# Channel attention and a squared-ReLU network on one core: the squares of batches 2 to 4 are summed by accumulating transfers instead of VectorE additions

## The chip, the cores and the metric

The kernel runs on one core of a Trainium2 chip. TensorE (PE) multiplies matrices, VectorE (DVE) and ScalarE (ACT) work elementwise, GpSimd (POOL) and SyncE (SP) here do little but issue transfers, which 16 DMA engines carry out. The metric is the device time of one execution in microseconds; three executions of the kernel before took 2157.32 to 2159.95 us, median 2158.8.

## What is computed

For each of four batches q, k and v are 6080 x 256. The columns of q and k are normalised over the 6080 rows, a 256 x 256 matrix of scores is made and put through a softmax, v is multiplied with it, and the result goes through two layers of 256 x 2048 and 2048 x 256 with a squared ReLU between them:

```python
qn = q / (np.linalg.norm(q, axis=1, keepdims=True) + 1e-06)
kn = k / (np.linalg.norm(k, axis=1, keepdims=True) + 1e-06)
s = kn.transpose(0, 2, 1) @ qn / tau
s = s - s.max(-1, keepdims=True)
a = np.exp(s)
a /= a.sum(-1, keepdims=True) + 1e-09
x = (v @ a).reshape(B * S, D)
r = np.maximum(x @ w_in, 0.0)
out = (r * r) @ w_out
```

The part that the change touches is the sum of squares inside the two norms: for each batch, 512 columns (256 of k, 256 of q), each summed over 6080 rows, which the host pads to 6144 = 128 x 48.

## The kernel before

**Tiles.** Batch b's q and k stand in one array of 128 partitions by 48 row blocks by 512 columns. `score_load` (L137) brings two row blocks at a time, a tile of 128 x 1024 values and 512 KB, on SyncE's queue; so a batch has 24 such tiles. `score_norm` (L144) squares a tile on ScalarE (L152) into a tile `sq` and VectorE adds it to the batch's running sum `acc` of 128 x 1024 (L153); the first tile of a batch is squared straight into `acc` (L149). That makes 23 squares and 23 additions in each batch. `score_split` (L155) splits the same tile for the score matmuls. `norms` (L197) adds the two halves of `acc` on VectorE (L199) and sums over the partitions on TensorE (L202); everything of the batch's attention follows from it.

**Buffers.** `sq` has the pool `work` with two buffers, and these two serve other steps under the same tag: the sums of weights in `weight_sums` (L508, its tile `f`), the combined tiles of `combine_sums` (L298), and the decoded weights at the start. A tile gets its buffer when all that read the buffer's last tile are done.

**Stages.** Batch 1's squares stand at the very start, before anything else can run. From then on the main loop goes through 192 quads (24 chunks of v by 8 pairs of hidden blocks); each quad is 7 products (m1 to m7, L440 to L498, matmuls at L384 of three passes each) and up to 8 products of the second layer (L550). m1 writes a bank that ScalarE copies (L447); m6 then adds to that same bank (L449), so it must follow the copy. m3's bank is evacuated by ScalarE (L394). ScalarE squares and casts (L395, L396, L418), VectorE subtracts the rounded part (L397, L419) and adds m7 (L472).

**Side work.** The attention of batches 2 to 4 is laid between the quads of the batch before, by a table of due times in quads (L705 to L733): `score_norm` of tile i is due 0.8 of a quad ahead of its matmuls; batch 2's first twelve are spread over quads 9 to 17 and the rest over quads 17 to 28, those of batches 3 and 4 over some 27 quads each, and `norms` 2 to 3 quads behind the last. `tie` (L769) keeps a side instruction from moving more than one quad ahead on TensorE, ScalarE and VectorE; within that, a scheduler sets the order on each engine, and every engine works its own list in order.

**GpSimd's queue.** Before the change it carries weights only: `wsc` (the folded weights, L318), `wins` and `wop` at the start, and in quads 9 to 13 the stores of `weight_sums` (L529), six for each of three weight blocks: `wodM` and `wos`, partly read from a tile `wo`, partly from a tile `hl` that VectorE has just made (L526).

Of the kernel before, what the change touches and what calls it, by code (L numbers as in the profile page):

```python
# [11 lines left out]
ALU = mybir.AluOpType  # L12
# [6 lines left out]
def tile_channel_attention_relu2_ffn(ctx, tc, kq, vT, tau, w_in, w_out, outT):  # L19

    nc = tc.nc
# [111 lines left out]
    accs = {}  # L133
# [10 lines left out]
    def score_norm(b, kt):  # L144

        x = kqt[b, kt // G]
        if kt == 0:
            accs[b] = small.tile([P, 2, C2], F32, name="acc")
            nc.scalar.activation(out=accs[b], in_=x, func=AF.Square)  # L149
        else:  # L150
            sq = work.tile([P, 2, C2], F32, name="sq", tag="sq")
            nc.scalar.activation(out=sq, in_=x, func=AF.Square)  # L152
            nc.vector.tensor_add(out=accs[b], in0=accs[b], in1=sq)  # L153

    def score_split(b, kt):  # L155
        x = kqt[b, kt // G]
# [484 lines left out]
    for g in range(NGK):  # L641
        for t in range(0, G, 2):
            score_norm(0, g * G + t)
        if g == NGK - 1:
            with tc.high_priority():
                norms(0)
        for t in range(G):
            kt = g * G + t
            score_mm(0, kt, s0, kt == 0, kt == NT - 1)
        if g == 4:  # L650
            load_tau()
        load_next()
# [53 lines left out]
    for b in range(1, B):  # L706
        u0 = (b - 1) * QB
        last = 30
        for i in range(NT // 2):
            k = 2 * i  # L710
            u = u0 + 2 + i * (last - 2) // (NT // 2)
            if b == 1:
                u = last - (NT - k) // 2 if k >= EARLY * G else NJ + 2 + 2 * i // 3
            if k % G == 0:
                at(u - 2.4, score_load, b, k // G)
            at(u - 0.8, score_norm, b, k)
            if b > 1 or k >= EARLY * G:
                at(u - 0.3, score_split, b, k)
                at(u + MID, score_burst, b, [k, k + 1])
        end = u0 + last  # L720
        at(end + MID, norms, b)
        at(end + 1 + MID, spread, b)
        at(end + 1.6, lambda b=b: exps(b, s_acc[b]))
        at(end + 2 + MID, attnT, b)
        for g in range(NG):
            u = end + 3 + 4 * g
            at(u - 1.5, load_win, b, g)
            at(u - 0.5, fold_split, b, g)
            at(u + MID, fold, b, g, 0)
            at(u + 1 + MID, fold, b, g, 1)  # L730
            at(u + 1.7, combine_sums, b, g)
            at(u + 1.71, combine_tile, b, g, 0)
            at(u + 2.7, combine_tile, b, g, 1)  # L733
# [60 lines left out]
    for n in range(len(quads) + 1):  # L794
        q = quads[n] if n < len(quads) else None
        p = quads[n - 1] if n else None
        for k, step in enumerate(plan):
            t = n + k / len(plan)
# [39 lines left out]
```

## Time and profile before

| | |
|---|---|
| median of three executions | 2158.8 us |
| the profiled execution, its own time | 2156.35 us |
| span in the profile, first to last instruction | 2154.6 us |
| granted TensorE clock, mean | 0.999 |
| HBM read and written | 381.16 and 63.31 MB |

The page gives busy times as shares of the span. They are averages over stages with different limits, so what a change in one stage is worth is read from that stage: from the chain of work that ended last in it, and from what the engines on that chain waited for. In the page's groups a row is line, engine, operation, output and inputs, count; behind the bar busy time and mean ns of one; behind the next the engine's idle time just ahead of it and what ended most of that.

### The profile page before, as it was taken

What the parts mean: (1) busy time and instruction counts of PE and PEld (TensorE: products, weight loads), DVE (VectorE), ACT (ScalarE), POOL (GpSimd) and SP (SyncE); (2) the same over time, 40 slices, a digit from 0 to 9 for tenths busy, and PEclk for the clock granted to TensorE, in tenths of its full rate; (3) what the DMA queues carried; (4) which work ended last, traced back from release to release, by engine and by line L of the source; (5) the groups of instructions that cost most, each with busy time, mean ns of one, the idle gap of its engine ahead of it and who ended that gap; (6) DMA issues with size and microseconds to landing.
All of it is one profiled execution on the core that took longest, in us unless ns stands there. A gap on an engine that the chain in (4) does not pass through costs nothing.

```text
span 2154.6 us, 27464 instructions
## 1 busy us (share of the span) xinstructions
PE 2139.2 (99%) x9758; PEld 1770.2 (82%) x9758; DVE 1733.2 (80%) x2492; ACT 1659.3 (77%) x2784; POOL 37.7 (2%) x69
## 2 busy tenths in 40 slices
PE   9999999999999999999999999999999999999999
PEld 8778888888888888888888888888888888888887
DVE  6898888787787988878779798897877877878876
ACT  6677778787787877877778878787777778778776
POOL 0111000000000000000000000000000000000000
PEclk9999999999999999999999999999999999999999
DMA  9768655355765655546667555554655654555542
GB/s 357 278 229 316 234 199 201 137 206 209 261 241 180 220 196 199 178 155 230 211 217 258 201 199 211 183 188 153 215 213 203 231 199 170 195 189 180 188 171 87
DMA packets 123176, 446.26 MB, mean 207 GB/s; under 512 B 12928, under 2 KB 29824, under 8 KB 123040
## 3 DMA queue, kind: packets, MB, share of 16 engines
q1 hardware_dynamic: 115744, 406.11, 53.3%
q0 software_dynamic: 7296, 38.41, 4.7%
q8 instruction: 77, 1.26, 0.2%
q14 instruction: 59, 0.48, 0.1%
HBM read 381.16 MB, written 63.31 MB: 206 GB/s over the span
## 4 chain that ended last, share of the span: by engine, by line
PE 94%; ACT 3%; DVE 2%; DMA 0%; issue 0%; SPq 0%; ACTq 0%; DVEq 0%
PE o L550 39%; PE h L384 23%; PE z L384 12%; PE h L550 6%; PE x L384 6%; PE h L173 4%; PE h L292 2%; PE x L173 2%; ACT g L418 0%; DVE s L472 0%; ACT r L394 0%; DMA kq<-kq 0%; DVE hl L85 0%; ACT r L395 0%; ACT g L396 0%
## 5 line engine op out<-in xcount | busy, mean ns | idle before, releaser
L550 PE MATMUL o<-g,wo 128*128 128x512 f32 (+1 forms) x3858 | 1003.9, 389 | 3.7 <-ACT g L418 2.4
L550 PEld LDWEIGHTS o<-g,wo 128*128 128x128 f32 x3858 | 719.3, 188 | 162.4 <-DVE g L419 10.8
L384 PE MATMUL h<-vt,wt 128*128 128x512 f32 (+1 forms) x2304 | 625.2, 389 | 1.2 <-ACT x L447 0.4
L384 PEld LDWEIGHTS h<-vt,wt 128*128 128x128 f32 x2304 | 430.8, 188 | 95.3 <-ACT uM L580 4.2
L397 DVE TENSOR_TENSOR g<-r,g 128x512 fp32r<-128x512 f32 (+1 forms) x384 | 260.6, 681 | 117.1 <-ACT g L396 114.7
L384 PE MATMUL z<-vt,wt 128*128 128x512 f32 (+1 forms) x1152 | 326.3, 390 | 0.9 <-DVE s L472 0.5
L419 DVE TENSOR_TENSOR g<-s,g 128x1024 fp32r<-128x1024 f32 (+1 forms) x142 | 172.1, 1212 | 119.4 <-ACT g L418 119.3
L394 ACT ACTIVATE r<-z 128x512 f32<-128x512 f32 (+1 forms) x192 | 113.5, 591 | 188.1 <-PE z L384 187.5
L384 PEld LDWEIGHTS z<-vt,wt 128*128 128x128 f32 x1152 | 209.9, 188 | 43.8 <-DVE s L472 4.5
L395 ACT ACTIVATE r<-r 128x512 f32<-128x512 f32 (+1 forms) x384 | 240.4, 629 | 5.9
L396 ACT CAST g<-r 128x512 fp32r<-128x512 f32 (+1 forms) x368 | 225.6, 616 | 5.2
L418 ACT CAST g<-s 128x1024 fp32r<-128x1024 f32 (+1 forms) x142 | 147.4, 1038 | 39.3 <-DVE s L417 39.1
L384 PE MATMUL x<-vt,wt 128*128 128x512 f32 (+1 forms) x576 | 161.9, 388 | 0.0
L455 ACT COPY z<-h 128x512 f32<-128x512 f32 (+1 forms) x192 | 110.9, 578 | 36.8 <-PE h L384 35.7
L384 PEld LDWEIGHTS x<-vt,wt 128*128 128x128 f32 x576 | 108.1, 188 | 21.7
L394 ACT ACTIVATE r<-x 128x512 f32<-128x512 f32 (+1 forms) x192 | 113.9, 593 | 14.5 <-DVE D L433 9.3
L153 DVE TENSOR_TENSOR acc<-acc,sq 128x1024 f32<-128x1024 f32 x92 | 112.2, 1220 | 15.6 <-ACT sq L152 13.5
L371 DVE TENSOR_TENSOR vt<-v,vt 128x512 fp32r<-128x512 f32 (+1 forms) x144 | 95.4, 681 | 35.8 <-ACT vt L370 35.7
L417 DVE SCALAR_TENSOR_TENSOR s<-s 128x1024 f32<-128x1024 f32 (+1 forms) x98 | 118.3, 1207 | 0.2
L447 ACT COPY x<-h 128x512 f32<-128x512 f32 (+1 forms) x192 | 111.5, 580 | 3.7 <-PE h L384 3.1
L467 ACT COPY m<-h 128x512 f32<-128x512 f32 (+1 forms) x192 | 111.6, 581 | 1.7 <-PE h L384 0.6
L472 DVE TENSOR_TENSOR s<-z,m 128x512 f32<-128x512 f32 (+1 forms) x142 | 96.6, 680 | 14.7 <-PE z L384 11.6
(154 smaller groups left out, 2406.5 us busy)
## 6 DMA issues: line engine op xcount, KB each, us to landing
wt<-wsc SPq DMA_DIRECT2D x184, 896.0 KB, 4.7
wo<-wop SPq DMA_DIRECT2D x134, 512.0 KB, 5.3
kq<-kq SPq DMA_DIRECT2D x87, 512.0 KB, 5.2
wsc<-wt POOLq DMA_DIRECT2D x32, 896.0 KB, 5.5
v<-vT SPq DMA_DIRECT2D x40, 512.0 KB, 5.2
outT<-uM SPq DMA_DIRECT2D x80, 256.0 KB, 3.3
wo<-wos SPq DMA_DIRECT2D x50, 384.0 KB, 3.5
wo<-wodM SPq DMA_DIRECT2D x64, 256.0 KB, 4.4
```

What stands on the lines that cost most here:

```text
L153: nc.vector.tensor_add(out=accs[b], in0=accs[b], in1=sq)
L173: nc.tensor.matmul(out=s[:, h * C:(h + 1) * C], lhsT=l, rhs=r, start=first and h == 0 and n == 0, stop=last and n == len(terms) - 1, skip_ ...
L384: nc.tensor.matmul(out=out[:, :T], lhsT=w[:, l, i], rhs=v[:, r, :T], start=start and n == 0, stop=n == 2, skip_group_check=True)
L394: nc.scalar.activation(out=r[:, :T], in_=ps[:, :T], func=AF.Relu)
L395: nc.scalar.activation(out=r[:, :T], in_=r[:, :T], func=AF.Square)
L396: eng(out=hl[:, 0, :T], in_=r[:, :T])
L397: nc.vector.tensor_sub(out=hl[:, 1, :T], in0=r[:, :T], in1=hl[:, 0, :T])
L417: nc.vector.scalar_tensor_tensor(out=s, in0=s, scalar=0.0, op0=ALU.max, in1=s, op1=ALU.mult)
L418: nc.scalar.copy(out=h, in_=s)
L419: nc.vector.tensor_sub(out=l, in0=s, in1=h)
L467: nc.scalar.copy(out=state[q]["m7"][:, :T], in_=H[:, :T])
L550: nc.tensor.matmul(out=o[:, :T], lhsT=l, rhs=r[:, :T], start=start and k == 0, stop=stop and k == 2)
```

## The change

The addition of L153 is kept for batch 1 alone. For batches 2 to 4 an accumulating transfer, issued from GpSimd's queue, adds `sq` to `acc` in place:

```diff
--- before.py
+++ after.py
@@ -150,7 +150,11 @@
         else:
             sq = work.tile([P, 2, C2], F32, name="sq", tag="sq")
             nc.scalar.activation(out=sq, in_=x, func=AF.Square)
-            nc.vector.tensor_add(out=accs[b], in0=accs[b], in1=sq)
+            if b:
+                nc.gpsimd.dma_start(out=accs[b].rearrange("p t c -> p (t c)"), in_=sq.rearrange("p t c -> p (t c)"),
+                                    accum_op=ALU.add)
+            else:
+                nc.vector.tensor_add(out=accs[b], in0=accs[b], in1=sq)
 
     def score_split(b, kt):
         x = kqt[b, kt // G]
```

Every line behind it has a number higher by 4 in the changed program. 69 additions (3 x 23) leave VectorE, and 69 transfers of 128 x 1024 values come to GpSimd's queue. In the rows below a number behind a name is that of the buffer's tile, and what stands in brackets is what the instruction waits for: DMASW with a number is a semaphore on which a transfer of GpSimd's queue lands, DMAHW one of SyncE's.

GpSimd's queue in batch 2, where the stores of `weight_sums` stand, before:

```order
L529 DMA wodM1_1491<-wo_1772 128x2x128 [waits DMAHW7_49,DMASW4_49]
L529 DMA wos4_1872<-wo_1772 256x1x256 [waits DMASW5_49]
L529 DMA wodM5_1492<-hl_1691 128x2x128 [waits DMASW6_49,DVE_49]
L529 DMA wodM6_1493<-hl_1691 128x2x128 [waits DMASW7_49]
L529 DMA wodM7_1494<-hl_1691 128x2x128 [waits DMASW0_49]
L529 DMA wos2_1684<-hl_1691 256x1x128 [waits DMASW1_49]
L529 DMA wodM5_1492<-hl_1879 128x2x128 [waits DMASW2_49,DVE_49]
L529 DMA wodM6_1493<-hl_1879 128x2x128 [waits DMASW3_49]
```

and in the changed program:

```order
L533 DMA wos4_1872<-wo_1772 256x1x256 [waits DMASW7_49]
L154 DMA acc_1531<-sq_1718 128x1024 [waits DMASW5_49,Activation_49]
L533 DMA wodM5_1492<-hl_1691 128x2x128 [waits DMASW1_49,DVE_49]
L533 DMA wodM6_1493<-hl_1691 128x2x128 [waits DMASW2_49]
L533 DMA wodM7_1494<-hl_1691 128x2x128 [waits DMASW3_49]
L533 DMA wos2_1684<-hl_1691 256x1x128 [waits DMASW4_49]
L154 DMA acc_1531<-sq_1721 128x1024 [waits DMASW0_49,Activation_49]
L154 DMA acc_1531<-sq_1806 128x1024 [waits DMASW6_49,DMASW5_49,Activation_49]
L154 DMA acc_1531<-sq_1910 128x1024 [waits DMASW7_49,DMASW6_49,Activation_49]
L154 DMA acc_1531<-sq_1913 128x1024 [waits DMASW7_49,Activation_49]
L533 DMA wodM5_1492<-hl_1879 128x2x128 [waits DMASW1_49,DVE_49]
```

Accumulations now stand between the stores, and each waits for the landing of the one before it: that of sq_1721 lands on DMASW5, for which that of sq_1806 waits, and so on through DMASW6 (sq_1806) and DMASW7 (sq_1910).

ScalarE at the same place, around the squares sq_1910 and sq_1913 (the sixth and seventh of batch 2), before:

```order
L152 ACTIVATE sq_1910<-kq_1759 128x1024 [waits DMAHW6_49]
L394 ACTIVATE r_1817<-x_1790 128x512 [waits PE_49]
L395 ACTIVATE r_1817<-r_1817 128x512 [waits Activation_49]
L152 ACTIVATE sq_1913<-kq_1761 128x1024 [waits DMAHW3_49,DVE_49]
L418 CAST g2_1840<-s_1832 128x1024 [waits DVE_49]
L394 ACTIVATE r_1863<-z_1812 128x512 [waits PE_49]
L525 CAST hl_1879<-sq_1873 128x512 [waits DMASW2_49,DMASW1_49,DMASW3_49,DMASW0_49,DVE_49]
L447 COPY x_1892<-h_1888 128x512 [waits PE_49]
L467 COPY m7_1898<-h_1894 128x512 [waits PE_49]
```

and in the changed program (L394 is now L398, L418 is L422, L447 is L451):

```order
L152 ACTIVATE sq_1910<-kq_1759 128x1024 [waits DMAHW6_49,DMASW6_49]
L398 ACTIVATE r_1817<-x_1790 128x512 [waits PE_49]
L399 ACTIVATE r_1817<-r_1817 128x512 [waits Activation_49]
L529 CAST hl_1879<-sq_1873 128x512 [waits DMASW3_49,DMASW2_49,DMASW4_49,DMASW1_49,DVE_49]
L152 ACTIVATE sq_1913<-kq_1761 128x1024 [waits DMAHW3_49,DMASW7_49]
L398 ACTIVATE r_1863<-z_1812 128x512 [waits PE_49]
L422 CAST g2_1840<-s_1832 128x1024 [waits DVE_49]
L451 COPY x_1892<-h_1888 128x512 [waits PE_49]
L399 ACTIVATE r_1863<-r_1863 128x512 [waits Activation_49]
L471 COPY m7_1898<-h_1894 128x512 [waits PE_49]
```

The square sq_1910 now waits for DMASW6, the landing of the accumulation of sq_1806, and sq_1913 for DMASW7, that of sq_1910: both tiles lie in one buffer. Before, sq_1910 waited for no more than its load and sq_1913 for VectorE's addition. The cast of `hl` has moved ahead of sq_1913; the evacuation of z, the cast to g2 and the copy of the bank h_1888 stand behind it as before.

VectorE at that place, before:

```order
L153 TENSOR_TENSOR acc_1531<-acc_1531,sq_1910 128x1024
L472 TENSOR_TENSOR s_1832<-z_1812,m7_1798 128x512
L472 TENSOR_TENSOR s_1832<-h_1786,m7_1798 128x512
L396 CAST g1_1818<-r_1817 128x512
L417 SCALAR_TENSOR_TENSOR s_1832<-s_1832 128x1024
L397 TENSOR_TENSOR g1_1818<-r_1817,g1_1818 128x512
L523 TENSOR_TENSOR sq_1873<-sq_1873 128x128
L153 TENSOR_TENSOR acc_1531<-acc_1531,sq_1913 128x1024
L419 TENSOR_TENSOR g2_1840<-s_1832,g2_1840 128x1024
L526 TENSOR_TENSOR hl_1879<-sq_1873,hl_1879 128x512
```

and in the changed program:

```order
L527 TENSOR_TENSOR sq_1873<-sq_1873 128x128
L400 CAST g1_1818<-r_1817 128x512
L476 TENSOR_TENSOR s_1832<-z_1812,m7_1798 128x512
L476 TENSOR_TENSOR s_1832<-h_1786,m7_1798 128x512
L401 TENSOR_TENSOR g1_1818<-r_1817,g1_1818 128x512
L421 SCALAR_TENSOR_TENSOR s_1832<-s_1832 128x1024
L530 TENSOR_TENSOR hl_1879<-sq_1873,hl_1879 128x512
L423 TENSOR_TENSOR g2_1840<-s_1832,g2_1840 128x1024
```

The two additions are gone, and the last piece of `f` (L523, now L527) and the split of `hl` (L526, now L530) have moved up by some places.

## The prediction

> **What bounds the kernel now.** I read the page first (shares, then the chain that ended last), then the busy time of TensorE in the stretches where the changed additions stand, then the chain in those stretches.
>
> ```profile
> span 2154.6 us, 27464 instructions
> PE 2139.2 (99%) x9758; PEld 1770.2 (82%) x9758; DVE 1733.2 (80%) x2492; ACT 1659.3 (77%) x2784; POOL 37.7 (2%) x69
> ...
> PE 94%; ACT 3%; DVE 2%; DMA 0%; issue 0%; SPq 0%; ACTq 0%; DVEq 0%
> ```
>
> TensorE is busy for 99% of the span, and 94% of the chain is its own matmuls following one another. VectorE works 80% of the time, but only 2% of the chain goes through it. The batches' squares stand in four stretches: batch 2 in 176 to 411 us (two rows of the view, since its DMA load falls off after 260), batch 3 in 616 to 937, batch 4 in 1147 to 1469. The view below gives TensorE's busy time in each; the last columns are the granted clock, the DMA engines' busy share and GB/s.
>
> ```profile
> 176.00:260.00 84.00, 84.00 (x372) 1.00 0.77 266
> 260.00:411.00 151.00, 150.95 (x727) 1.00 0.53 187
> ...
> sum 878.00, PE 877.47; mean PE 219.37
> ```
>
> TensorE is idle there for 878.00 - 877.47 = 0.5 us in all. Busy is not the same as fastest, so I asked for the chain of these stretches too (first row 260 to 411, second 616 to 937; batch 4's reads like batch 3's):
>
> ```profile
> by line: PE o L550 38.2%; PE h L384 22.9%; PE z L384 12.5%; PE h L173 11.4%; PE h L550 6.7%; PE x L384 5.4%; issue 0.5%; ACT r L395 0.4%; ACT r L394 0.4%; ACT z L455 0.4%; ACT g L396 0.3%; ACT m L467 0.3%; ACT x L447 0.3%; ACT uM L616 0.3%;
> by line: PE o L550 39.1%; PE h L384 24.1%; PE z L384 12.0%; PE h L173 10.7%; PE x L384 6.2%; PE h L550 5.6%; ACT g L418 0.6%; ACT r L395 0.4%; ACT g L396 0.4%; ACT r L394 0.4%; ACT uM L580 0.3%; ACT x L447 0.3%; issue 0.1%
> ```
>
> No VectorE piece is named in either; what is not TensorE is ScalarE, about 2.4%.
>
> **What the change takes away.** The group of the removed additions, its time within the same four stretches, and the waits between the square and the addition (us in total, times, longest):
>
> ```profile
> L153 DVE TENSOR_TENSOR acc<-acc,sq 128x1024 f32<-128x1024 f32 x92 | 112.2, 1220 | 15.6 <-ACT sq L152 13.5
> ...
> sum 878.00, DVE 84.04; mean DVE 21.01
> ```
>
> ```profile
> DVE acc L153 <- ACT sq L152: 13.5, 14, 8.7
> ACT sq L152 <- DVE acc L153: 4.1, 13, 0.7
> ```
>
> Of the 92 additions 23 are batch 1's and stay; 69 x 1.22 us = 84 us leave VectorE, which the second row confirms. As VectorE is not on the chain there, these 84 us lie wholly under TensorE. What can come back is only what VectorE delays through ScalarE. Its ceiling is the ScalarE share: 2.4% of 151 + 321 + 322 us = 19 us, if every one of those pieces vanished; its floor is nothing; and the scheduler's new order around the gaps could also cost, by as little. Idle TensorE time (0.5 us) is the nearer row, because ScalarE keeps all its own work. I credit **1 us**, and let the range reach to 5.
>
> **What it adds.** 69 transfers of 512 KB from GpSimd's queue, each an accumulation into the same tile, so each is issued only after the one before has landed; and each square now waits until the accumulation that reads its buffer has landed, where it waited for a 1.2 us addition. The price is the time from issue to landing, call it L. No accumulating transfer is in this trace. The nearest rows are the plain writes of that queue and its packet time (packets, MB, share of 16 engines; then KB each and median us to landing):
>
> ```profile
> q0 software_dynamic: 7296, 38.41, 4.7%
> ...
> wop<-wo POOLq DMA_DIRECT2D x8, 512.0 KB, 5.8
> wins<-sq POOLq DMA_DIRECT2D x3, 512.0 KB, 2.9
> wodM<-hl POOLq DMA_DIRECT2D x9, 128.0 KB, 6.2
> ```
>
> The same size from the same queue landed in 2.9 us at best and 5.8 us as a rule; the small pieced writes that stand in the very stretch 176 to 260 took 6.2. In engine time 4.7% of 2154.6 us for 38.41 MB makes 1.4 us for 512 KB. An accumulation must read its destination as well, so at least one more such pass: 2.9 + 1.4 = 4.3 us undisturbed, 5.8 + 1.4 = 7.2 us in traffic. The ends I keep are 2.9 (no extra cost) and 10 (5.8 and three more passes). I take **L = 5.8**, the row of equal size and queue, which is also the middle of 4.3 and 7.2. The Trainium skill, "DMA: Bandwidth & Descriptors", section "Anatomy of one DMA", has a fit for this queue of about 2.0 us plus bytes over 436 GB/s; for 512 KB that is an estimate of 3.2 us, near the best row here and well under the usual one, and by it the sum below would have no loss at all. It has no price for accumulation, so the rows decide.
>
> The issue itself is cheap: GpSimd is busy 37.7 us in all. Traffic grows by 69 x 0.52 = 36 MB beside 446 MB:
>
> ```profile
> DMA packets 123176, 446.26 MB, mean 207 GB/s; under 512 B 12928, under 2 KB 29824, under 8 KB 123040
> ...
> wt<-wsc SPq DMA_DIRECT2D x184, 896.0 KB, 4.7
> ```
>
> SP's largest loads land in 4.7 us and are issued 1.5 quads ahead (192 quads in the span, so over 15 us); the 8% more traffic lies beside that lead.
>
> **Where the new wait bites.** In batch 2 the first squares come fast, and three groups of weight stores share GpSimd's queue with them. The rows: GpSimd's stores, then ScalarE from the fifth square (204.28) to the copies that TensorE needs, then TensorE.
>
> ```profile
> 201.65 2.12 POOL L529 DMA_DIRECT2D wodM<-hl  x3 [7.52 <-DVE hl L526]
> 203.76 0.71 POOL L529 DMA_DIRECT2D wos<-hl  x1
> ```
>
> ```profile
> 204.28 1.06 ACT L152 ACTIVATE sq<-kq 128x1024 f32<-128x1024 f32 x1
> ...
> 215.58 1.07 ACT L152 ACTIVATE sq<-kq 128x1024 f32<-128x1024 f32 x1
> ...
> 218.50 1.06 ACT L152 ACTIVATE sq<-kq 128x1024 f32<-128x1024 f32 x1 [0.70 <-DVE acc L153]
> 221.16 1.06 ACT L418 CAST g<-s 128x1024 fp32r<-128x1024 f32 x1 [1.60 <-DVE s L417]
> 222.12 0.58 ACT L394 ACTIVATE r<-z 128x512 f32<-128x512 f32 x1
> 222.61 0.61 ACT L525 CAST hl<-sq 128x512 fp32r<-128x512 f32 x1
> 223.12 0.58 ACT L447 COPY x<-h 128x512 f32<-128x512 f32 x1
> ```
>
> ```profile
> 223.06 1.52 PE L550 MATMUL o<-g,wo 128*128 128x512 f32 x6
> 224.42 0.84 PE L384 MATMUL h<-vt,wt 128*128 128x512 f32 x3
> ```
>
> The order of the changed program (above, both places) says who waits. On GpSimd the accumulation of sq_1721 stands behind the `wos` store, so it is issued at 203.76 + 0.71 = 204.5 and lands at 204.5 + L. That of sq_1806 (squared at 204.28) waits for it and lands at 204.5 + 2L. ScalarE's square sq_1910, at 215.6 before, waits for that landing; it ends 1.1 us later and its own accumulation lands L after. Square sq_1913, at 218.5 before, reuses the same buffer at once and waits for that. So sq_1913 starts at T = the later of 216.6 + L and 205.6 + 3L. Queued behind it on ScalarE are the evacuation of z (L394), the cast L418 and the copy of m1's bank (L447). From start to start these rows take 1.0, 0.5 and 1.0 us, and the copy 0.6, so the copy ends at T + 3.0. TensorE's three matmuls at 224.42 add to the bank that this copy reads, so they cannot start sooner. The loss is therefore T + 3.0 - 224.4 wherever that is positive: it begins at L = 4.8 (T = 221.4). At L = 5.8, T = 205.6 + 17.4 = 223.0 and the loss is **1.6 us**. At 4.3 it is 0, at 7.2 it is 5.8, at 10 it is 14.
>
> Later squares have more room. Batches 3 and 4 alternate two buffers and nothing else uses GpSimd's queue; their closest squares are these of batch 3:
>
> ```profile
> 701.54 1.06 ACT L152 ACTIVATE sq<-kq 128x1024 f32<-128x1024 f32 x1
> 706.75 1.06 ACT L152 ACTIVATE sq<-kq 128x1024 f32<-128x1024 f32 x1
> 718.96 1.05 ACT L152 ACTIVATE sq<-kq 128x1024 f32<-128x1024 f32 x1
> 727.19 1.06 ACT L152 ACTIVATE sq<-kq 128x1024 f32<-128x1024 f32 x1
> ```
>
> The square at 718.96 needs the accumulation issued at 702.6 landed: L up to 16. The one at 727.19 needs the second of two in a row: 702.6 + 2L, so L up to 12. Below that, no wait. What reads the finished sums, L199, comes late enough (batch 2's 23 squares, batch 3's, then batch 2's L199; first and last start):
>
> ```profile
> L152 ACT ACTIVATE sq<-kq x23: 1052/1062/1077, 177.2 to 376.2; 128x1024 f32<-128x1024 f32 x23
> ...
> L152 ACT ACTIVATE sq<-kq x23: 1051/1061/1071, 616.1 to 901.2; 128x1024 f32<-128x1024 f32 x23
> ...
> L199 DVE TENSOR_TENSOR acc<-acc x1: 684/684/684, 403.9 to 403.9; 128x512 f32<-128x512 f32 x1
> ```
>
> From 376.2 to 403.9 there are 27.7 us for one or two landings.
>
> **The sum.** The profiled execution took 2156.35 us (span 2154.6 and 1.75 around it); -1 for VectorE, +1.6 for sq_1913, gives 2156.95. The median shown is 2158.8, which is 2.45 above the profiled execution; on that footing I forecast **2159.4 us**. Only a change of over 0.2%, 4.3 us, can be told from none in this kernel.
>
> **The rivals.**
>
> *The landing is slow enough to push batch 2 (slower).* The same wait with L from 7 to 10: for it, the DMA engines are 77% busy in 176 to 260 and the small writes there took 6.2; against it, 2.9 us is possible. Decided at L = 6.7, where the loss 3 x 6.7 + 205.6 + 3.0 - 224.4 = 4.3 reaches the mark. It gives 2163 to 2182 us, the upper end for L = 10 (14 us, and an estimated 8 for two more squares of that crowd that would wait about 4 each). Chance 0.22.
>
> *The chain of accumulations becomes the pace.* If L is over 12, every square of batches 3 and 4 waits too. At L = 15, 23 x 15 = 345 us do not fit between the first and last square of batch 2 (199 us by the rows above) nor of batches 3 and 4 (285 each): 146 + 60 + 60 = 266 us, so about 2420. Only the missing row for an accumulation allows it; chance 0.12.
>
> *VectorE holds off GpSimd's descriptors (slower).* A mechanism of this kernel would be that VectorE, 80% busy, delays each issue on GpSimd. The row against it, ns of one issue:
>
> ```profile
> L318 POOL DMA_DIRECT2D wsc<-wt x32 | 17.1, 534 | 1479.1 <-DVE wt L316 1479.1
> ```
>
> Thirty-two issues at a mean of 534 ns beside that same VectorE show no such delay. Were 2.5 us added to each L (8.3), the loss would be 205.6 + 24.9 + 3.0 - 224.4 = 9 us, 2167. The Trainium skill, "SBUF — State Buffer", in its passage on VectorE blocking DMA under "SBUF: two separate sides", names this stall for transfers issued from GpSimd; the trace does not bear it out. Chance 0.04.
>
> *VectorE's relief counts (faster).* ScalarE waits less for VectorE, and a quarter or more of the 19 us goes: 2154 or less. For it, the ScalarE pieces on the chain; against, no VectorE piece beside them. Chance 0.08. That the additions stay where they were is excluded: the new order lists none of the 69 on VectorE.
>
> **How the numbers follow.** Forecast, within 0.2%: 0.54 (L from 2.9 to 6.7). Slower: 0.22 + 0.12 + 0.04 = 0.38. Faster: 0.08. The range 2154 to 2182 leaves out the chain case and about half of the faster one, 0.16 and a little.
>
> **What will show it.** VectorE's busy time near 1649 us, 69 accumulations on GpSimd, 36 MB more in its queue; their median landing between 4.3 and 7.2; ScalarE waiting for an accumulation at the seventh square of batch 2 for a few us, TensorE late by 1 to 2 us behind it, and no such wait in batches 3 and 4. A median landing over 6.7, or waits of squares past 600 us, would prove me wrong.

## The result, and the profile after

| | before | after |
|---|---|---|
| median | 2159.01 us | 2177.26 us (four executions, 2176.59 to 2178.33) |
| ratio, 95% interval | | 1.0086 (1.0068 to 1.0103) |
| profiled execution, its own time | 2156.35 us | 2178.33 us |
| span | 2154.6 us | 2176.6 us |
| granted TensorE clock, mean | 0.999 | 0.996 |

The change costs 18.3 us, 0.86%, well over what a measurement can tell from none. The time lies inside the predicted range, but the case forecast as likeliest, no change, did not come; the rival with the slow landing in batch 2 did. The two profiled executions differ by 22.0 us, since the one of before was 2.7 us under its median and the one of after 1.1 us over.

On the page of the changed kernel, the lines that answer to those of before:

```profile
span 2176.6 us, 27570 instructions
PE 2149.6 (99%) x9758; PEld 1773.3 (81%) x9758; DVE 1660.2 (76%) x2423; ACT 1659.7 (76%) x2784; POOL 97.3 (4%) x138
...
q0 software_dynamic: 17232, 74.59, 13.5%
...
PE 85%; ACT 2%; DMA 2%; DVE 0%; issue 0%
...
acc<-sq POOLq DMA_DIRECT2D x69, 512.0 KB, 6.5
```

All that was to be moved has moved: 69 instructions less on VectorE, 73 us less of its busy time, 36.2 MB and 69 issues more on GpSimd's queue. Yet TensorE's share still reads 99%: part of the loss is hidden in it, since its busy time is 10.4 us longer for the same matmuls. The new entry is DMA with 2% of the chain that ended last (this page follows the chain back only to 219 us, so its shares sum to 90% and PE's 85% cannot be set beside the 94% of before). The windows of the four stretches show where it was lost (busy time of PE, PEld, DVE, ACT, POOL with instruction counts, granted clock, DMA share, GB/s):

```profile
176.00:260.00 84.00, 74.23 (x301) 59.07 (x300) 46.87 (x74) 48.29 (x76) 18.05 (x23) 0.93 0.92 280
260.00:411.00 151.00, 150.95 (x715) 124.88 (x715) 117.49 (x160) 122.22 (x197) 11.98 (x14) 0.99 0.81 247
616.00:937.00 321.00, 320.02 (x1527) 265.80 (x1526) 249.11 (x344) 256.82 (x416) 20.77 (x25) 1.00 0.77 241
1147.00:1469.00 322.00, 320.88 (x1532) 266.73 (x1531) 249.16 (x344) 257.84 (x417) 20.74 (x25) 1.00 0.77 240
```

Where TensorE was busy for all of 84.00 us at clock 1.00 before, it is now idle for 9.8 us, and the mean clock is 0.93, with some of the low clock left in the next row, at 0.99. Both programs have 9758 matmuls, so the start of the n-th can be compared: the one that starts at 176 us before comes 1.4 us late after the change, the one at 260 us 18.3 us late. That is 16.9 us of the 22.0 lost in one stretch. Batches 3 and 4 show 2.1 us of idle time together, where all four stretches had 0.5 before. The 1.4 us were lost ahead of 150 us, before the first accumulation of the stretch is issued (179.9), and so not by it: the trace shows 3.41 us at half clock there, which that of before does not have.

Now the stretch itself. What engines waited for in 170 to 300 us (total us, times, longest), and the time from issue to landing of the accumulations there:

```profile
POOL acc L154 <- DMA acc<-sq: 25.7, 4, 8.2
ACT sq L152 <- DMA acc<-sq: 18.0, 6, 4.7
DVE g L400 <- ACT r L399: 16.3, 5, 7.6
...
PE z L388 <- DVE s L476: 7.2, 2, 4.0
```

```profile
DMA to landing us min/median/max: 5.4/7.7/10.1
```

ScalarE's squares wait six times for an accumulation, and TensorE stands behind VectorE's addition of m7. Later, in batches 3 and 4, no square waits at all: the 18.0 us are all that the whole trace has. The largest of the early stops, engine by engine (start, duration, engine, line; what the engine was idle for just before in brackets): ScalarE,

```profile
219.72 0.57 ACT L459 COPY z<-h 128x512 f32<-128x512 f32 x1
224.99 1.06 ACT L152 ACTIVATE sq<-kq 128x1024 f32<-128x1024 f32 x1 [4.69 <-DMA acc<-sq]
...
226.56 0.63 ACT L399 ACTIVATE r<-r 128x512 f32<-128x512 f32 x1
...
232.22 1.06 ACT L152 ACTIVATE sq<-kq 128x1024 f32<-128x1024 f32 x1 [4.52 <-DMA acc<-sq]
```

VectorE,

```profile
227.22 0.43 DVE L400 CAST g<-r 128x512 fp32r<-128x512 f32 x1 [4.57 <-ACT r L399]
227.56 0.68 DVE L476 TENSOR_TENSOR s<-z,m 128x512 f32<-128x512 f32 x1
```

and TensorE:

```profile
222.93 2.20 PE L554 MATMUL o<-g,wo 128*128 128x512 f32 x9
228.30 1.65 PE L388 MATMUL z<-vt,wt 128*128 128x512 f32 x3 [3.18 <-DVE s L476]
229.75 1.48 PE L554 MATMUL o<-g,wo 128*128 128x512 f32 x3
231.03 2.76 PE L388 MATMUL h<-vt,wt 128*128 128x512 f32 x6
```

The sixth square of batch 2, sq_1910, could start after the copy at 219.72 but waits 4.69 us for a landing. The rounding steps of the next tile stand behind it on ScalarE; VectorE's cast of that tile (L400) is its next instruction and waits 4.57 us; the addition of m7 (L476), which could have run, is queued behind the cast; and TensorE's z needs that addition. Before the change VectorE's order had both additions of m7 ahead of that cast. The seventh square, where the prediction looked for the loss, waits 4.52 us too, until 232.22, but TensorE is working through that time. Both squares wait for the landing of the accumulation right before them, not of the one before that: the pair's other buffer is taken by `f` of `weight_sums` then (VectorE writes it from 220.44 us on, under the name `sq`).

It works at half speed. The row at 228.30 takes 1.65 us for three matmuls, where three took 0.84 before. The windows of TensorE over that gap (busy time, clock, DMA share, GB/s):

```profile
220.00:224.00 4.00, 4.00 (x19) 1.00 0.99 253
224.00:228.00 4.00, 1.13 (x5) 0.96 0.27 59
228.00:232.00 4.00, 3.70 (x9) 0.50 0.88 206
232.00:236.00 4.00, 4.00 (x14) 0.69 0.43 110
236.00:240.00 4.00, 4.00 (x19) 1.00 1.01 280
```

The granted clock is 0.50 from 227.7 us, just before the gap of 3.2 us ends, to 234.5: 6.83 us, of which TensorE works 6.2 at half speed and so loses another 3.1. A second gap of 4.0 us at 252, of the same form (the tenth square waits 4.67 us), comes with another 6.83 us, of which 5.6 are worked, a loss of 2.8.

### The profile page after: what moved, and what is told of

Same layout as the page of the kernel before. It is cut to its first block, busy times and chain, and to the rows that moved or that the text cites. A ratio compares the mean times of both kernels' runs of the same rounds, so it can differ in the third digit from the quotient of the medians.

```text
span 2176.6 us, 27570 instructions
## 1 busy us (share of the span) xinstructions
PE 2149.6 (99%) x9758; PEld 1773.3 (81%) x9758; DVE 1660.2 (76%) x2423; ACT 1659.7 (76%) x2784; POOL 97.3 (4%) x138
## 3 DMA queue, kind: packets, MB, share of 16 engines
q0 software_dynamic: 17232, 74.59, 13.5%
## 4 chain that ended last, share of the span: by engine, by line
PE 85%; ACT 2%; DMA 2%; DVE 0%; issue 0%
PE o L554 36%; PE h L388 21%; PE z L388 11%; PE h L554 6%; PE x L388 5%; PE h L177 4%; PE h L296 2%; DMA wt<-wsc 1%; DMA acc<-sq 1%; ACT g L422 0%; ACT r L398 0%; ACT r L399 0%; DVE s L476 0%; ACT sq L152 0%; ACT g L400 0%
## 5 line engine op out<-in xcount | busy, mean ns | idle before, releaser
L388 PE MATMUL z<-vt,wt 128*128 128x512 f32 (+1 forms) x1152 | 328.6, 393 | 10.6 <-DVE s L476 7.6
L398 ACT ACTIVATE r<-z 128x512 f32<-128x512 f32 (+1 forms) x192 | 113.5, 591 | 188.7 <-PE z L388 188.1
L400 ACT CAST g<-r 128x512 fp32r<-128x512 f32 (+1 forms) x368 | 225.8, 617 | 5.4
L422 ACT CAST g<-s 128x1024 fp32r<-128x1024 f32 (+1 forms) x142 | 147.3, 1038 | 39.6 <-DVE s L421 39.4
L459 ACT COPY z<-h 128x512 f32<-128x512 f32 (+1 forms) x192 | 110.9, 578 | 36.2 <-PE h L388 35.0
L398 ACT ACTIVATE r<-x 128x512 f32<-128x512 f32 (+1 forms) x192 | 113.9, 593 | 13.8 <-DVE D L437 8.6
L451 ACT COPY x<-h 128x512 f32<-128x512 f32 (+1 forms) x192 | 111.5, 581 | 6.8 <-PE h L388 6.2
L476 DVE TENSOR_TENSOR s<-z,m 128x512 f32<-128x512 f32 (+1 forms) x142 | 96.7, 681 | 14.2 <-PE z L388 11.0
L152 ACT ACTIVATE sq<-kq 128x1024 f32<-128x1024 f32 x80 | 84.8, 1060 | 23.5 <-DMA acc<-sq 18.0
```

The costliest lines, as they stand in the source:

```text
L388: nc.tensor.matmul(out=out[:, :T], lhsT=w[:, l, i], rhs=v[:, r, :T], start=start and n == 0, stop=n == 2, skip_group_check=True)
L398: nc.scalar.activation(out=r[:, :T], in_=ps[:, :T], func=AF.Relu)
L400: eng(out=hl[:, 0, :T], in_=r[:, :T])
L422: nc.scalar.copy(out=h, in_=s)
L451: nc.scalar.copy(out=st["X"][:, :T], in_=st["B"][:, :T])
L459: nc.scalar.copy(out=st["Z"][:, :T], in_=st["B"][:, :T])
```

## The experiments

All edits are to the changed kernel. In the expectations, W is the theory that the waits of batch 2's crowded squares for their buffer, with what is queued behind them, are the loss; T is that the added traffic slows every load a little, everywhere. P was formed after the first seven runs: the chain of accumulations, each waiting for the landing of the last, is slower than the squares come in that stretch, and whoever stands behind a buffer it holds is stopped. Ratios are to the kernel before, run on the same chip, with 95% intervals.

### Which batch, and what part of the transfer

Only batch 2 by accumulating transfers, batches 3 and 4 by VectorE as before:

```diff
-            if b:
+            if b == 1:
```

> Accumulating transfers for batch 2 alone; batches 3 and 4 add on VectorE again. Theory W (ScalarE stands at squares whose buffer an accumulation still reads, only where batch 2's squares are crowded, and TensorE idles and then runs at half clock): nearly the whole loss stays, 2175 to 2178 us, with two TensorE gaps of 3 to 4 us between 220 and 260 us. Theory T (the doubled packet time of 36 MB loads the DMA engines and delays SyncE's loads everywhere, loss in proportion to the transfers): a third of it, about 2165.

Measured: 2177.69 us, ratio 1.0098 (1.0081 to 1.0115). A third of the transfers (50.47 MB in the queue in place of 74.59) cost all of the loss, and the waits of 150 to 420 us are those of the full change:

```profile
ACT sq L152 <- DMA acc<-sq: 17.8, 6, 4.8
...
PE z L388 <- DVE s L476: 6.9, 2, 4.0
```

Only batches 3 and 4:

```diff
-            if b:
+            if b > 1:
```

> The other half: batch 2 adds on VectorE, batches 3 and 4 by accumulating transfers. Theory W: 2159 to 2163 us (about 1 and 1.5 us were lost in each of those two batches in the changed kernel's trace), no square of them waits over 1 us. Theory T: two thirds of the loss, about 2171.

Measured: 2160.42 us, ratio 1.0005 (0.9996 to 1.0014). Forty-six accumulations cost nothing that can be told, and the 46 x 1.22 = 56 us that they take off VectorE gain nothing. Their landing is hardly quicker than over the whole of the full change (median 6.5):

```profile
DMA to landing us min/median/max: 4.5/6.4/10.7
```

So T falls, by both runs, and what differs between the batches is the spacing (and somewhat the landing, 6.4 us here against 7.7 in batch 2's crowd): batch 3's 23 squares stand 13 us apart (616.1 to 901.2), batch 2's first thirteen 7.3 us (177.2 to 264.7 before the change, over twelve steps).

The same 69 transfers without the addition:

```diff
-                nc.gpsimd.dma_start(out=accs[b].rearrange("p t c -> p (t c)"), in_=sq.rearrange("p t c -> p (t c)"),
-                                    accum_op=ALU.add)
+                nc.gpsimd.dma_start(out=accs[b].rearrange("p t c -> p (t c)"), in_=sq.rearrange("p t c -> p (t c)"))
```

> Plain writes in place of accumulating ones (the running sum is overwritten, so the norms of batches 2 to 4 are of the last tile alone); same queue, same chain of waits, same order. If the size of the landing decides (packets of 159 ns in place of 327): landings of 4 to 5 us, the squares wait less, 2159 to 2165 us. If the waiting in GpSimd's queue or the two buffers as such decide whatever the transfer costs: 2172 or more.

Measured: 2165.16 us, ratio 1.0033 (1.002 to 1.0046): two thirds of the loss are gone with the addition, a third stays. Its queue and landing on the page, and its waits in 150 to 420 us:

```profile
q0 software_dynamic: 17232, 74.59, 9.0%
...
acc<-sq POOLq DMA_DIRECT2D x69, 512.0 KB, 4.5
```

```profile
ACT sq L152 <- DMA acc<-sq: 8.2, 3, 3.7
```

The same packets and bytes take 9.0% of the DMA engines where accumulating takes 13.5%. Against the 4.7% of before, the added 9936 packets take (0.090 x 2162.8 - 0.047 x 2154.6) x 16 / 9936 = 0.15 us each as plain writes and (0.135 x 2176.6 - 0.047 x 2154.6) x 16 / 9936 = 0.31 us accumulating. The addition doubles the time of a packet, and the median landing goes from 4.5 to 6.5 us. The order of instructions is that of the changed kernel on TensorE, ScalarE, VectorE and GpSimd, one by one, so the new order by itself does not cost the 18 us. What keeping the old order of VectorE would win with accumulations was not tried. With the shorter landing no gap of TensorE in 176 to 260 us was over 1.73 us, and its clock stayed at 1.00.

### Take the wait from ScalarE, or spread the squares

If only ScalarE's wait mattered, freeing it should win everything back. First, the accumulation reads the loaded tile itself, so that the square's buffer is free at once:

```diff
-            nc.scalar.activation(out=accs[b], in_=x, func=AF.Square)
+            nc.scalar.activation(out=accs[b], in_=x, func=AF.Square, scale=1000.0 if b else 1.0)
...
-                nc.gpsimd.dma_start(out=accs[b].rearrange("p t c -> p (t c)"), in_=sq.rearrange("p t c -> p (t c)"),
+                nc.gpsimd.dma_start(out=accs[b].rearrange("p t c -> p (t c)"), in_=x.rearrange("p t c -> p (t c)"),
```

> The accumulating transfers read the loaded tile instead of its square (so the raw values are summed, and the first square of batches 2 to 4 is scaled by a million); the square's buffer is free at once, while the transfers, their chain and their packets stay. Theory W: the stops at squares are gone and with them 14 us or more, 2158 to 2164 us. Theory T: 2175 to 2179.

Measured: 2174.77 us, ratio 1.0081 (1.0066 to 1.0096). W's number was missed; T's (2175 to 2179) was nearly met, though the wait found below is not T's. Second, batch 2's early squares are written over the loaded tile:

```diff
-            sq = work.tile([P, 2, C2], F32, name="sq", tag="sq")
+            sq = x if b == 1 and kt < EARLY * G else work.tile([P, 2, C2], F32, name="sq", tag="sq")
```

> The first twelve tiles of batch 2, which nothing else reads, are squared in place, so that the accumulation holds one of the four buffers of loaded tiles in place of one of the two square buffers; all 69 transfers stay and the result is the full computation. Theory W: the crowd no longer stops ScalarE, 2158 to 2164 us; if the loads behind those four buffers come late, a few us more. Theory T: 2175 to 2179.

Measured: 2182.04 us, ratio 1.0108 (1.0093 to 1.0123), a miss of both numbers, and no faster than the change itself. Both free ScalarE and stop someone else. In the second, SyncE's queue in 170 to 300 us, its issues, and TensorE in 150 to 420:

```profile
SPq L141 <- DMA acc<-kq: 85.2, 11, 10.6
```

```profile
265.76 0.38 SPq L335 DMA_DIRECT2D wt<-wsc  x1
274.94 0.33 SPq L141 DMA_DIRECT2D kq<-kq  x1
...
282.92 0.38 SPq L335 DMA_DIRECT2D wt<-wsc  x1
```

```profile
PE h L388 <- DMA wt<-wsc: 13.8, 3, 7.0
```

Now the accumulation holds a buffer of the loads. `score_load` (L141) waits for it eleven times, up to 10.6 us, in a queue that works in order, and the quads' weights (L335) behind it come 17 us apart; TensorE waits for them. In the first of the two SyncE waited 88.3 us and TensorE 10.9. The wait is not ScalarE's own: it belongs to the transfer, and goes where the buffer goes.

The twelve early tiles an even two thirds of a quad apart in place of whole quads:

```diff
-                u = last - (NT - k) // 2 if k >= EARLY * G else NJ + 2 + 2 * i // 3
+                u = last - (NT - k) // 2 if k >= EARLY * G else NJ + 2 + 2 * i / 3
```

> Batch 2's early squares are due every two thirds of a quad, about 6.8 us apart, in place of pairs at one time. If pairs are what overruns the two buffers: half of the loss or more goes, 2160 to 2168 us. If the mean spacing is below what a chain of landings of 8 to 10 us allows: little changes, 2172 to 2180.

Measured: 2180.14 us, ratio 1.0103 (1.0088 to 1.0118). Squares still waited 17.4 us in all, five times, up to 7.5. That fits the second case: evening out does not help where the mean spacing is what is short.

The weight stores of `weight_sums` moved from GpSimd's queue to SyncE's:

```diff
-            nc.gpsimd.dma_start(out=out, in_=x.bitcast(F32))
+            nc.sync.dma_start(out=out, in_=x.bitcast(F32))
```

> The weight stores of weight_sums go to SyncE's queue, so that nothing but accumulations stands in GpSimd's queue in that stretch. If the stores hold the accumulations back (the issue of the second one waited for them until 189.4 us in the changed kernel): the stops shrink by 2 to 6 us in all, 2168 to 2175 us, unless SyncE's own loads wait behind the stores. If the chain of landings alone decides: within 2 us of 2177.

Measured: 2175.44 us, ratio 1.008 (1.0063 to 1.0097), not to be told from the change. Nothing stands between the accumulations any more, but the squares wait as long, up to 6.3 us each, and the longest landing is 10.5:

```profile
ACT sq L152 <- DMA acc<-sq: 18.0, 6, 6.3
```

The stores, which the prediction put at the head of its sum, are not the cause in the changed kernel.

### Room against pace

A third buffer for the early squares. There is no free memory for one; they take the three of the tag D, which the quads use later:

```diff
-            sq = work.tile([P, 2, C2], F32, name="sq", tag="sq")
+            tag, n = ("D", DB) if b == 1 and kt < EARLY * G else ("sq", 2)
+            sq = work.tile([P, 2, C2], F32, name=tag, tag=tag, bufs=n)
```

> Batch 2's first eleven squares get the three buffers of the tag D, which nothing else uses before quad 16, in place of one or two of sq; all 69 accumulations stay, none holds a buffer of the loads, and the result is the full computation. Theory P (the pace: a chain of landings of about 8 us against squares every 7.4 us, which any buffer behind it stops sooner or later, on ScalarE with the tag sq, on SyncE's queue with the loaded tiles): the backlog of 11 x 0.6 to 1 us = 7 to 11 us, one tile or one and a half, fits into three buffers, ScalarE waits under 2 us in all, 2159 to 2163 us. Theory T (the transfers as such delay the weight loads in that stretch): TensorE waits for wt, 2170 or more.

Measured: 2166.59 us, ratio 1.0033 (1.0021 to 1.0045): 7.9 us lost in place of 18.3. P's 2159 to 2163 was missed by 4 us, and the waits of TensorE for `wt` that T expected did not come. The squares wait 5.4 us in all, and TensorE's windows (busy, clock, DMA share, GB/s) lose nothing up to 230 us:

```profile
176.00:200.00 24.00, 24.00 (x107) 1.00 1.01 337
200.00:230.00 30.00, 30.00 (x135) 1.00 1.01 330
230.00:260.00 30.00, 27.20 (x114) 0.94 0.90 249
```

The accumulations themselves were hardly quicker (7.3 us in the median). The squares also no longer share a pair with `f`, and the run does not tell the one from the other. With D and the pair of `sq` together, two of the eleven squares in the latter:

```diff
-            sq = work.tile([P, 2, C2], F32, name="sq", tag="sq")
+            tag, n = ("D", DB) if b == 1 and kt < EARLY * G and kt % 8 else ("sq", 2)
+            sq = work.tile([P, 2, C2], F32, name=tag, tag=tag, bufs=n)
```

> As the run with three buffers, and every fourth early square of batch 2 in sq: four buffers in turn. Theory P: with three, ScalarE still waited 5.4 us in all and TensorE stood 3.0 us once, because the chain lagged by two tiles; a fourth buffer takes that up, ScalarE waits under 1.5 us, no half clock behind 150 us, 2160 to 2163 us, no more than 2 us over the kernel that accumulates for batches 3 and 4 alone (2160.4). If what is left over 2159 is the transfers' load on SyncE's loads: 2165 or more, with TensorE waiting for wt or wo.

Measured: 2171.04 us, ratio 1.0057 (1.0044 to 1.007), over P's 2160 to 2163, and without the waits for `wt` or `wo` of the other case. TensorE in the crowded stretch, then the waits of 120 to 420 us:

```profile
176.00:200.00 24.00, 24.00 (x108) 1.00 1.02 339
200.00:230.00 30.00, 30.00 (x134) 1.00 0.98 325
230.00:260.00 30.00, 30.00 (x133) 1.00 0.93 274
```

```profile
PE z L389 <- DVE D L477: 7.2, 2, 5.3
ACT sq L153 <- DMA acc<-sq: 6.5, 1, 6.5
...
DVE D L477 <- DMA acc<-D: 3.1, 1, 3.1
```

With room enough, the stretch that lost 17 us loses nothing, with landings of 8.5 us in the median. But room only defers: the chain is behind by then. When the quads ask for D again, at 261 us, VectorE waits 3.1 us for an accumulation and TensorE 1.8 for VectorE. At 284 us a square with the tag `sq` waits 6.5 us, and what is queued behind it on ScalarE and VectorE stops TensorE for 5.3, as in the changed kernel.

The early squares spread from an earlier start, 0.92 of a quad apart:

```diff
-                u = last - (NT - k) // 2 if k >= EARLY * G else NJ + 2 + 2 * i // 3
+                u = last - (NT - k) // 2 if k >= EARLY * G else 7 + 0.92 * i
```

> Batch 2's early squares start three quads sooner and are due every 0.92 of a quad, about 9.4 us apart; buffers as in the changed kernel. Theory P: a landing of 8 us fits into 9.4 us, the stops shrink to 2 to 4 us, no half clock, 2160 to 2166 us. If two buffers stop ScalarE whatever the spacing: 2172 or more.

Measured: 2177.4 us, ratio 1.0083 (1.007 to 1.0097). P's number was missed, and the other case's was met: the landings between 120 and 300 us, 9.4 us in the median, are among the slowest of these runs, and one square's wait of 10.2 us makes one stop of 9.7 at 189 us in place of four small ones:

```profile
DMA to landing us min/median/max: 6.2/9.4/10.5
```

```profile
ACT sq L152 <- DMA acc<-sq: 21.8, 5, 10.2
...
PE z L388 <- ACT z L459: 10.5, 2, 9.7
```

The stores have a part in that stop. The accumulation for which the square waits belongs to a square that ended at 180.8 us, but on GpSimd it stands behind a store that waits for a load of `wo`, and it is issued at 187.3 and lands at 197.2:

```profile
186.01 0.72 POOL L533 DMA_DIRECT2D wodM<-wo  x1 [9.44 <-DMA wo<-wop]
...
187.32 1.07 POOL L154 DMA_DIRECT2D acc<-sq  x1
```

The wider spacing with the stores on SyncE's queue was not tried, so this run does not decide on P. It shows that the landing is no constant of the chain. I took the load on the DMA engines for its reason (a share of 1.0 at the start of the stretch) and halved the second loads of those tiles, one row block in place of two, each squared twice:

```diff
+        if b == 1 and g < EARLY and tag == "kq" and (1, g) in kqt:
+            nc.sync.dma_start(out=t[:, :1], in_=kq[b, :, g * G:g * G + 1, :])
+            kqt[b, g] = t[:, 0:1].to_broadcast([P, G, C2])
+            return
```

> The changed kernel, but the second loads of batch 2's first twelve tiles bring one row block in place of two (the squares take it twice, so the other row block is left out of the norm): 12 x 256 KB less on the DMA engines in 176 to 260 us, everything else alike. If the engines' fullness (share 1.01 in 176 to 200 us, 0.92 in 200 to 230) makes the landings 8 to 10 us there: landings fall by 1 us or more in the median, the stops at squares from 18 to under 10 us, 2163 to 2170 us. If the accumulation itself takes 8 us whatever else runs: within 3 us of 2177.

Measured: 2178.17 us, ratio 1.0085 (1.0067 to 1.0103). The first case was missed. The number is the second's, but an accumulation does not take 8 us whatever else runs (6.4 in batches 3 and 4). The landing stays at 7.4 us in the median, and the share at the start of the stretch falls little (0.98 in 176 to 200 us where it was 1.01, 0.81 in 200 to 230 where it was 0.92). Half of these loads were not what fills the engines, or not enough of it. The squares still waited 19.1 us in all. What makes a landing 8 to 10 us there stays open.

### GpSimd adds, without a transfer

```diff
-                nc.gpsimd.dma_start(out=accs[b].rearrange("p t c -> p (t c)"), in_=sq.rearrange("p t c -> p (t c)"),
-                                    accum_op=ALU.add)
+                nc.gpsimd.tensor_add(out=accs[b], in0=accs[b], in1=sq)
```

> GpSimd adds the squares of batches 2 to 4 itself, with its own instruction in place of the transfers: VectorE is relieved of the same 84 us, and no landing and no DMA traffic is added. If VectorE's relief is worth the 1 us that the prediction credits, and GpSimd adds a tile in less than the 7 us between squares: 2156 to 2160 us. If it is worth a quarter of ScalarE's 19 us on the chain: 2154 or less. If GpSimd's addition is slow (over 7 us) or holds VectorE off: squares wait for it in batch 2, 2165 or more.

Measured: 2224.45 us, ratio 1.031 (1.0296 to 1.0324), the worst of all, although the chain is short: an addition takes 2.4 us in the median, no landing behind it. GpSimd's first, then VectorE at that moment, then the group of VectorE's subtractions on the page:

```profile
178.38 2.67 POOL L154 TENSOR_TENSOR acc<-acc,sq 128x1024 f32<-128x1024 f32 x1 [12.57 <-ACT sq L152]
```

```profile
178.71 3.42 DVE L420 SCALAR_TENSOR_TENSOR s<-s 128x1024 f32<-128x1024 f32 x1
```

```profile
L400 DVE TENSOR_TENSOR g<-r,g 128x512 fp32r<-128x512 f32 (+1 forms) x384 | 308.2, 806 | 129.9 <-ACT g L399 127.4
```

VectorE's step, 1.21 us elsewhere, takes 3.42 and ends 1.1 us behind GpSimd's addition, as if it had begun only at that one's end. The subtractions grow from 682 to 806 ns in the mean. The Trainium skill, "SBUF — State Buffer", section "SBUF: two separate sides", says that VectorE and GpSimd lock a shared pair of ports against each other for a whole instruction, if VectorE's has two inputs in SBUF and GpSimd's reads SBUF, as both do here; these rows agree. So GpSimd is no free adder beside a VectorE that is 80% busy. None of the versions beat the kernel before.

## Why the prediction came out as it did

**What bounds the kernel, and VectorE's relief.** Right. The additions' group fell from 112.2 to 28.2 us, the 84.0 of the prediction, and TensorE gained nothing from it; the credit of 1 us is within what the run with batches 3 and 4 alone leaves (0.9996 to 1.0014). VectorE's busy time fell by 73 us only, 1660.2 against 1649: neighbouring instructions overlap in the records by some 0.08 us at either end, so a group's sum is more than what it adds to the busy time.

**The mechanism and the place.** Right: squares of batch 2 wait for the accumulation that holds their buffer, and batches 3 and 4 do not. Right also that in batches 3 and 4 the traffic by itself costs nothing to be measured.

**The landing, L = 5.8: the step that failed.** It was taken from plain writes of equal size. The median of all 69 is 6.5, inside the 4.3 to 7.2 that was looked for, but in the stretch that decides it is 7.7, over the 6.7 from which the prediction itself gave the case to its rival. For a plain write 5.8 was about right there: without the addition the same transfers landed between 170 and 300 us in

```profile
DMA to landing us min/median/max: 2.9/5.6/8.2
```

What was left out is the addition. The prediction had the term, one more pass of 1.4 us for the read of the destination, which the packets bear out (0.31 us accumulating against 0.15 plain), and its own figure with it was 7.2 in traffic. Instead it took 5.8, the row of equal size without the pass, because it was also the middle between quiet and traffic; but the stretch is all traffic, and the addition cost 7.7 - 5.6 = 2.1 us there.

**Where it was priced.** One square, the seventh, was priced, with the queue behind it on ScalarE. In the trace the second, third, fifth, sixth, seventh and tenth wait, and what stops TensorE longest are the sixth and the tenth (3.2 and 4.0 us), whose own waits were not in the sum: their lateness goes through VectorE's cast to the addition of m7 behind it. The new order on VectorE, with the cast ahead of that addition, was known, but only ScalarE's queue was followed. The start of the sum was early too: it let the fourth accumulation (sq_1721) go at 204.5, behind the stores, but that one had to wait for the landing of the third at 209.3 as well:

```profile
209.84 0.90 POOL L154 DMA_DIRECT2D acc<-sq  x1 [3.91 <-DMA acc<-sq]
```

At L = 7.7 the formula gives 205.6 + 23.1 + 3.0 - 224.4 = 7.3 us, all of it at the seventh square. TensorE's idle time in the stretch was 9.8, in four stops behind the second, third, sixth and tenth; so the landing alone does not make up the 18 us.

**The clock.** Missing from the sum. The half clock that came with the two gaps of over 3 us cost 3.1 + 2.8 = 5.9 us more. With 9.8 + 5.9 = 15.7 the two account for nearly all of the 16.9.

**The rivals.** The slow landing came true, at 2177 in its 2163 to 2182, and the two more squares with waits of about 4 us each that its upper end allowed for did come (4.69 and 4.67). That the time fits is in part luck: at L = 7.7 the rival's formula alone gives 2159.4 - 1.6 + 7.3 = 2165, and the rest came from other stops and from the clock. The chain did become the pace, as the second rival said, but in the crowded stretch alone, since batches 3 and 4 leave it 13 us for each tile. That VectorE holds off GpSimd's issues by 2.5 us shows in no row: one accumulation's issue took 847 to 1077 ns in that stretch, 0.3 to 0.5 us more than the 534 of a plain one.

## What to carry to other kernels

A chain of transfers that each wait for the last has a pace, its landing in that very stretch under load; compare it with the spacing of what feeds it there, not over the whole kernel. Where it is slower, more or other buffers only choose who stops, an elementwise engine, a load queue with weights behind it, or a later reader; more room helps just as long as the lag fits into it. Work taken from an engine that is not on the chain buys nothing, so any new wait in exchange is a loss.

## What the runs showed of the hardware

**A gap of TensorE can cost again.** After short gaps the granted clock falls to half, for 3.41, 6.83 or 10.24 us, always a multiple of 3.41 (one behind the last matmul is cut off by the end). In the fourteen profiles here every gap of TensorE from 2.80 us up came with such a spell: 2.80 us with 3.41, the 3.18 and 3.98 of the changed kernel with 6.83 each, 9.73 with 10.24. Of the gaps between 1.0 and 2.6 us only some did. A gap of 1.48 us at 136 us stands in all fourteen and was followed by 3.41 us at half clock in eight, the changed kernel's among them and not that of before, so a microsecond or two of a difference between two profiles can be this alone. The Trainium skill, "TensorE: Matmul & The Clock Gate", section "Part 1: The HAM clock gate (the "warmup" mystery)", gives a free-running window of about 3.4 us and half rate after an idle window. The multiples agree with it; that a gap shorter than a window already does it, 1.48 us here, goes beyond what it says.

**A landing has no fixed size.** In the changed kernel the same 512 KB accumulation landed in 4.5 to 10.8 us. While TensorE stood, the loads stood too (DMA share 0.27 at 224 to 228 us above), so a stop may itself let the chain catch up; that was not tried.
